# Key loads in 1 KB packets with head-wise turning, first scores in halves, and a re-ordered plan

## The chip, the cores and the metric

One core of one Trainium2 chip runs the program. The metric is the device time of one execution in microseconds (us). Lower is better. The kernel before was timed three times: 790.86, 791.15 and 791.73 us, median 791.15.

## The reference

Three stages follow each other, all in float32.

```python
scores = scale * np.matmul(q, k.transpose(0, 1, 3, 2))      # q, k, v: (2, 8, 576, 64)
kth = np.partition(scores, -32, axis=-1)[..., -32:-31]
scores = np.where(scores >= kth, scores, -1000000000.0)
attn = np.exp(scores - np.max(scores, axis=-1, keepdims=True))
attn = attn / (np.sum(attn, axis=-1, keepdims=True) + 1e-09)
x = np.matmul(attn, v)                                      # -> (1152, 512)

p = domain_probs / (domain_probs.sum(-1, keepdims=True) + 1e-09)
for e in range(4):                                          # w1 (4, 512, 1024), w2 (4, 1024, 512)
    out += p[:, e:e + 1] * (np.maximum(x @ w1[e], 0.0) @ w2[e])

y = ((out @ w_a) * (out @ w_b)) @ w_out                     # (512, 1536), (512, 1536), (1536, 512)
```

Each row of scores keeps only its 32 largest entries. Then come four experts, all applied to all tokens, and a gated pair of matrix products.

## The kernel before, in words

The 1152 tokens are cut into nine tiles of 128. They form four groups of 1, 2, 3 and 3 tiles (`GROUPS`). Attention works in 36 **steps**: for each group, for each pair of heads, for each tile. Step 0 to 3 are the one tile of group 0, steps 4 to 11 the two tiles of group 1.

A step goes through these stages:

- **Scores** (`scores`, TensorE): four matmuls of 288 columns for two heads, into two PSUM slots (`atts`, two of them). ScalarE copies them to SBUF (L813).
- **Selection** (`masked`, VectorE): the 32 largest of each row, eight at a time, by MAX8 (L842) and MATCH_REPLACE8 (L859). Steps 0 to 11 fold the row into two halves of 288 columns first, the later steps work on 576.
- **Softmax** (`masked`): GpSimd makes the limits (L905, L909), ScalarE the mask (L915) and the exponential with its sum (L920), GpSimd adds 1e-9 to the two sums (L925), VectorE takes the reciprocal (L928), ScalarE scales (L931).
- **Turning** (`weigh`, TensorE, "the turn" below): after a small GpSimd memset (L950), nine transposes into both `atts` slots. ScalarE copies them out (L977).
- **Values** (`weigh`, TensorE, "AV" below): ten matmuls of 64 output rows for each tile, into PSUM bank 7 (`os_`). ScalarE (and VectorE, for the groups of several tiles) takes the result away as `xf` (group 0, L1005) or `xs` (L1011, L1013).

The rows of keys come by `keys`: one DMA for the main part of a pair of heads (four blocks of 128 rows), one load of the remaining rows for all heads, six transposes (L689) and one copy by ScalarE (L705). Keys of batch 0 are turned in the first 20 us, those of batch 1 (`keys(1, prep, n + 2.0)`) during steps 1 to 6, and are kept in DRAM for the later groups. The first key load has its own path: its block copies are split between ScalarE (L701) and VectorE (L702).

Between these, TensorE does the experts of the groups already attended (`plain` for group 0 in float32, `experts` for the others in split float32r) and at last the gated products (`gated`). Before any of this work exists, 150 **filler** matmuls on zeros (`FILL`, `ps<-xs 128x256`) stand in the holes. They write into an `ms` slot, one of three PSUM banks that group 0's experts also use, and hold it until the last of them.

The order in which each engine's instructions stand is fixed when the kernel is built. `Plan` is a list scheduler: every piece of work has an engine, an assumed duration, a **key** (the smaller goes first among the pieces that are ready), its waits and its buffers. `AHEAD` sets the key of the scores (`n - AHEAD`), `SLACK` is an assumed delay after the sums of the softmax, `SINCE` gives the earliest assumed time of group 0's four wide weight loads. The planner tries 42 orders with small random delays and keeps one. On the chip each engine takes its own instructions strictly in that order, and DMAs of SyncE (SP) are issued in order too.

Of the kernel before, what the change touches and what calls it, by code (L numbers as in the profile page):

```python
# [29 lines left out]

AHEAD = 4.4
OPERANDS = 5.0
# [361 lines left out]
def dve(n):  # L394
    return 62 + 1.04 * n
# [18 lines left out]
FILL = 150  # L414
SLACK, EASE = 1200, 600

# [10 lines left out]
EARLY, WIDE = 4, 4  # L427
SINCE = 20e3, 25e3, 30e3, 40e3


def body(tc, q, k, v, probs, w1, w2, wa, wb, wo, out):
# [227 lines left out]
    def keys(b, h2, key):  # L659

        h = 2 * h2
        rt, kt = kraws.tile(key), kts.tile(key)
        rv = lambda: rt.ap.rearrange("p (m h d) -> p m h d", h=2, m=M4)
        first_ = not krem_done
        lds = [load(rv, lambda: pair_rows(k, b, h), key - 2, (), [rt])]

# [12 lines left out]
        else:  # L679
            done = krem_done[0]  # L680
        at = atts.tile(key + 0.02)
        kr = lambda i: krem0[(1 - b, b)[i]].ap if first_ else krem[(1 - b, b)[i]].ap[:, h * D:(h + 2) * D]
        krs = krem0 if first_ else krem

        def turn(blocks):
            a = at.ap.rearrange("p c n -> p (c n)")
            for i in blocks:
                src = kr(i // (M4 + 1)) if i % (M4 + 1) == 0 else rt.ap[:, (i - 1) * 128:i * 128]
                tr(a[:, i * 128:(i + 1) * 128], src, ident)  # L689

        if first_:

            o = tensor(3 * TURN_F, lambda: turn((1, 2, 3)), key + 0.02, lds + [ready], [at, rt])
            o = tensor(TURN_F, lambda: turn((0,)), key + 0.021, [o, done[0], done[3]], [at] + krs)
            o2 = tensor(2 * TURN_F, lambda: turn((4, 5)), key + 0.022, [o] + done, [at, rt] + krs)
        else:
            o = tensor(6 * TURN_F, lambda: turn(range(M4 + 2)), key + 0.02, lds + done + [ready], [at, rt] + krs)
        av = lambda c0, c1: at.ap.rearrange("p c n -> p (c n)")[:, REM + c0:REM + c1]
        if first_:
            got = [  # L700
                scalar(512 - REM, lambda: nc.scalar.activation(kt.ap[:, 0:512 - REM], av(0, 512 - REM), AF.Copy), -902, [o], [at, kt]),  # L701
                vector(dve(2 * REM + 64), lambda: nc.vector.tensor_copy(kt.ap[:, 512 - REM:WK], av(512 - REM, WK)), -902, [o2], [at, kt]),  # L702
            ]
        else:
            got = [scalar(WK, lambda: nc.scalar.activation(kt.ap, av(0, WK), AF.Copy), -902, [o], [at, kt])]  # L705
        if any(c for c, g in enumerate(GROUPS) if (b, h2) not in kept and c >= 0):
# [9 lines left out]
    def queries(pair, n, key):  # L716
# [19 lines left out]
        if MIX in pair.tiles:  # L736
# [3 lines left out]
            lds += qrem_done  # L740
        at = ms.tile() if n == 0 else atts.tile(key + 0.04)
        a = lambda: (at.ap if n == 0 else at.ap[:, 0])[:, 0:T * 128]
# [49 lines left out]
    def scores(pair, i, n):  # L792

        t = pair.tiles[i]
        ats, ss_ = [atts.tile(n - AHEAD + 0.001 * j) for j in range(2)], [scores_slot(n + 0.001 * j * (1 if n else -1)) for j in range(2)]
        parts = [(slice(0, 128), t[0])] if t != MIX else [(slice(b * REM, (b + 1) * REM), b) for b in range(B)]

        def emit():
            for c in range(2):
                for j in range(2):  # L800
                    for rs, b in parts:
                        c0 = (1 - j) * REM + c * HALF
                        mm(
                            ats[j].ap[rs, c, 0:HALF], pair.q.ap[j * D:(j + 1) * D, i * 128 + rs.start:i * 128 + rs.stop],
                            pair.k[b].ap[j * D:(j + 1) * D, c0:c0 + HALF], start=True, stop=True,
                        )

        o = tensor(SCORE / 2 + TILED, emit, n - AHEAD, pair.qd + sum((pair.kd[b] for _, b in parts), []), ats + [pair.q] + [pair.k[b] for _, b in parts])
        got = []
        for j in range(2):  # L810
            at, s = ats[j], ss_[j]
            ev = scalar(
                S, lambda s=s, at=at: nc.scalar.activation(s.ap.rearrange("p (c n) -> p c n", c=2), at.ap[:, :, 0:HALF], AF.Copy),  # L813
                -2000 + n, [o], [at, s],
            )
            got.append((s, ev, at, o))
        return got

    def masked(sd, n):
# [91 lines left out]
        for x in range(2):  # L911
# [12 lines left out]
            ))  # L924
        sm = gpsimd(290, lambda: nc.gpsimd.tensor_scalar(sums.ap, sums.ap, 1e-9, None, op0=ALU.add), -500, ex, [sums])  # L925

# [11 lines left out]
    def weigh(pair, i, ed, n):  # L938
# [46 lines left out]
        def emit():  # L985
# [11 lines left out]
        pair.od = [tensor(  # L997
            T * AV + SWITCH, emit, n + 0.6, [zeroed] + sum((d for _, _, d in pair.turned), []) + sum((pair.vd[b] + vrem_done[b] for b in bs), []),
            [pair.o] + [p for _, p, _ in pair.turned] + [pair.v[b] for b in bs],
# [491 lines left out]

    idle = ms.tile()
    steps = [(c, h2, i) for c, g in enumerate(GROUPS) for h2 in range(HP) for i in range(len(g))]
# [11 lines left out]
    for i in range(FILL):  # L1505
        late = i >= 150
        op = tensor(
            120, lambda: mm(idle.ap[:, 0:256], zeros_[:, 0:128], zeros_[:, 128:384], start=True, stop=True),
            1e9 + i, [blank], [idle],
        )  # L1510
# [33 lines left out]
```

## Time and profile before

| what | us |
|---|---|
| median of three runs | 791.15 |
| the profiled execution's own time | 791.33 |
| span of its profile, first to last instruction | 789.5 |
| TensorE (PE) busy | 779.3 |
| VectorE (DVE) busy | 710.3 |
| ScalarE (ACT) busy | 504.6 |
| GpSimd (POOL) busy | 324.3 |

The profiled execution's time is 1.8 us above its span and 0.18 us above the median. A busy PE is not a PE at its peak: matmuls are pipelined and overlap, so what one costs is read from the distance between the starts of equal ones and not from its own length. A float32 matmul of the program appears as two in the profile.

### The profile page before, as it was taken

Reading aid. Unit: us, or ns where it says so; the run is one execution under the profiler, and the core shown is the slowest. Engines: PE = TensorE matmul, PEld = TensorE weight load, DVE = VectorE, ACT = ScalarE, POOL = GpSimd, SP = SyncE. Lnnn points to the kernel's source line nnn. Section 1 sums busy time; section 2 is a strip of 40 time slices with the busy share of each in tenths; the row PEclk is TensorE's granted clock in tenths of the full one; section 3 lists DMA queues with packets and bytes.
Section 4 is the critical chain, followed back from the end, with each engine's and each line's share of the span. In section 5 each row is a group of like instructions: output and inputs, shape, how many; then the busy total and the mean of one; then the engine's idle time right before and its main releaser. Section 6 shows DMA issues by size and latency. Waiting matters only on the chain.

```text
span 789.5 us, 14542 instructions
## 1 busy us (share of the span) xinstructions
PE 779.3 (99%) x5286; PEld 684.7 (87%) x5286; DVE 710.3 (90%) x1548; ACT 504.6 (64%) x871; POOL 324.3 (41%) x353
## 2 busy tenths in 40 slices
PE   9989999999999999999999999999999999999997
PEld 8877676888888888889998999998898989999896
DVE  6999999999999999999939998999786899898655
ACT  3888888999888898787765566666436424241010
POOL 4354423568575534546445122232314424343120
PEclk9999999999999999999999999999999999999999
DMA  6867976756556524324345558896311331311013
GB/s 157 257 221 240 304 213 207 216 170 186 156 166 186 168 71 134 107 82 135 106 160 161 177 163 315 275 321 216 107 54 54 107 103 59 107 54 54 1 54 120
DMA packets 99464, 121.35 MB, mean 154 GB/s; under 512 B 26560, under 2 KB 73664, under 8 KB 97856
## 3 DMA queue, kind: packets, MB, share of 16 engines
q1 hardware_dynamic: 98976, 120.33, 48.4%
q8 instruction: 41, 0.67, 0.3%
q14 instruction: 31, 0.25, 0.1%
q10 hardware_dynamic: 416, 0.10, 0.1%
HBM read 109.14 MB, written 11.27 MB: 153 GB/s over the span
## 4 chain that ended last, share of the span: by engine, by line
PE 75%; DVE 21%; DMA 1%; issue 1%; POOL 1%; ACT 0%; DVEq 0%; POOLq 0%; SPq 0%
PE ps L597 72%; DVE low L842 9%; DVE e L859 7%; PE ps L600 3%; DVE e L882 1%; DMA e<-in_moe_w_b_dram 1%; DMA raw<-in_moe_w_dram 0%; DVE rest L1440 0%; DVE low L1440 0%; POOL mid_again L1035 0%; DVE low L1387 0%; DVE mid_again L1107 0%; POOL rest L1443 0%; DVE low L893 0%; DVE big_again L1394 0%
## 5 line engine op out<-in xcount | busy, mean ns | idle before, releaser
L597 PE MATMUL ps<-mid_again 128*128 128x512 f32 x1092 | 261.4, 393 | 0.0
L597 PEld LDWEIGHTS ps<-mid_again 128*128 128x128 f32 x1092 | 201.6, 188 | 42.2 <-issue 1.6
L597 PE MATMUL ps<-xs,mid_again 128*128 128x384 f32 (+1 forms) x1152 | 192.2, 320 | 0.7 <-DVE mid_again L1107 0.7
L597 PEld LDWEIGHTS ps<-xs,mid_again 128*128 128x128 f32 x1152 | 181.3, 189 | 8.0 <-issue 4.7
L1035 POOL TENSOR_TENSOR mid_again<-raw,mid_again 128x1024 fp32r<-128x1024 f32 x64 | 154.1, 2415 | 50.5 <-ACT mid_again L1034 49.6
L842 DVE MAX8 low<-e 128x8 f32<-128x576 f32 (+1 forms) x285 | 160.7, 599 | 0.0
L1351 POOL TENSOR_TENSOR low<-e,e 128x512 int32<-128x512 int32 x36 | 61.3, 1702 | 146.2 <-DVE e L1348 85.5
L1034 ACT ACTIVATE mid_again<-raw 128x1024 fp32r<-128x1024 f32 x96 | 101.9, 1063 | 20.9 <-PE ps L597 11.2
L859 DVE MATCH_REPLACE8 e<-low,e 128x576 f32<-128x576 f32 (+1 forms) x190 | 112.0, 594 | 0.0
L597 PE MATMUL ps<-xs,big_again 128*128 128x320 f32 (+1 forms) x576 | 86.4, 297 | 0.1
L597 PEld LDWEIGHTS ps<-xs,big_again 128*128 128x128 f32 x576 | 80.4, 190 | 1.1 <-DVE low L1440 0.3
L597 PE MATMUL ps<-lowa_again,big_again 128*128 128x320 f32 (+1 forms) x432 | 66.7, 297 | 1.0 <-ACT rest L1449 0.8
L1103 ACT ACTIVATE mid_again<-ps 128x384 fp32r<-128x384 f32 (+1 forms) x96 | 43.8, 457 | 31.5 <-PE ps L597 30.0
L597 PEld LDWEIGHTS ps<-lowa_again,big_again 128*128 128x128 f32 x432 | 60.6, 190 | 2.6 <-ACT rest L1449 1.1
L931 ACT ACTIVATE e<-e,low 128x576 f32<-128x576 f32 x72 | 52.9, 773 | 11.7 <-DVE low L928 11.4
L920 ACT ACTIVATE e<-e,low 128x576 f32<-128x576 f32 x72 | 55.8, 779 | 0.2
L1107 DVE SCALAR_TENSOR_TENSOR mid_again<-ps,mid_again 128x384 fp32r<-128x384 f32 (+1 forms) x96 | 48.1, 502 | 7.2 <-ACT mid_again L1103 6.7
L1440 DVE TENSOR_TENSOR low<-ps,low 128x256 f32<-128x256 f32 (+1 forms) x105 | 43.5, 444 | 11.9 <-PE ps L597 11.4
L1443 POOL TENSOR_TENSOR low<-low 128x256 f32<-128x256 f32 (+1 forms) x30 | 28.5, 950 | 59.6 <-DVE low L1440 58.4
L597 PE MATMUL ps<-big 64*128 64x288 f32 (+1 forms) x320 | 46.6, 427 | 1.7 <-ACT lowa L977 1.7
L977 ACT ACTIVATE lowa<-ps 128x512 f32<-128x512 f32 x72 | 42.8, 646 | 5.0 <-PE ps L600 4.9
L1035 DVE TENSOR_TENSOR mid_again<-raw,mid_again 128x1024 fp32r<-128x1024 f32 x32 | 40.7, 1277 | 4.3 <-ACT mid_again L1034 3.9
(125 smaller groups left out, 1101.5 us busy)
## 6 DMA issues: line engine op xcount, KB each, us to landing
raw<-in_moe_w_dram SPq DMA_DIRECT2D x116, 512.0 KB, 4.0
low<-in_v_dram SPq DMA_DIRECT2D x24, 256.0 KB, 3.5
e<-in_moe_w_b_dram SPq DMA_DIRECT2D x12, 512.0 KB, 3.8
e<-in_moe_w_a_dram SPq DMA_DIRECT2D x12, 512.0 KB, 4.1
e<-in_moe_w_out_dram SPq DMA_DIRECT2D x12, 512.0 KB, 5.2
wscr<-big_again SPq DMA_DIRECT2D x6, 1024.0 KB, 7.3
mid_again<-wscr SPq DMA_DIRECT2D x6, 1024.0 KB, 4.8
big<-kscr SPq DMA_DIRECT2D x16, 320.0 KB, 3.3
```

The lines of the kernel that those rows point to most:

```text
L597: nc.tensor.matmul(out, l, r, **kw)
L842: 62 + 1.04 * width, lambda at=at, cs=cs: nc.vector.max(m8v()[:, x, cs], at()), key + 0.02 * r, done if isinstance(done, list) else [done],
L859: lambda at=at, cs=cs, to=to: nc.vector.match_replace(out=to(), in_to_replace=m8v()[:, x, cs], in_values=at(), imm_value=LOW),
L920: lambda x=x: nc.scalar.activation(ev(x), ev(x), AF.Exp, bias=endv()[:, x, 0:1], accum_out=sums.ap[:, x:x + 1]),
L931: S, lambda x=x: nc.scalar.activation(ev(x), ev(x), AF.Copy, scale=sums.ap[:, x:x + 1]),
L977: w, lambda j=j, w=w, at=at: nc.scalar.activation(p.ap[:, j * MAIN:j * MAIN + w], at.ap.rearrange("p b n -> p (b n)")[:, j * (MAIN - 128): ...
L1034: hi = scalar(1024, lambda: nc.scalar.activation(u.ap[:, 0:1024], r.ap, AF.Copy), 500 + s, [ld], [u, r], sbuf=True)
L1035: sub = lambda eng: eng.tensor_tensor(u.ap[:, 1024:2048], r.ap, u.ap[:, 0:1024], op=ALU.subtract)
L1103: n, lambda h=h, p=p: nc.scalar.activation(h.ap[:, 0:n], p.ap[:, 0:n], AF.Relu), -1000, [o], [h, p]
L1107: lambda h=h, p=p: nc.vector.scalar_tensor_tensor(h.ap[:, n:2 * n], p.ap[:, 0:n], 0.0, h.ap[:, 0:n], op0=ALU.max, op1=ALU.subtract),
L1351: return gpsimd(pool_(512), lambda: nc.gpsimd.tensor_tensor(t().bitcast(I32), fold(c.ap.bitcast(I32)), fold(lowv().bitcast(I32)), op=ALU.a ...
L1440: return vector(dve(m), lambda: nc.vector.tensor_tensor(tv(out), p.ap[:, 0:m], tv(i), op=ALU.add), K, [o] + after, [p, tp])
```

## The change

- The main part of a pair of keys is loaded head by head, `main_rows` in place of `pair_rows`. Four rows of one head lie together in DRAM, so a packet is 1 KB instead of 256 B.
- In the new layout a block's two heads do not lie side by side. So each of the four main blocks is turned by two matmuls against the identity, one for each head, that write 64 rows each, in place of one transpose of 128 rows. The two blocks of remaining rows keep their transpose.
- For the first keys the turned blocks lie in two `ms` slots, not in an `atts` slot.
- Step 0's scores are two pieces: the first 288 columns wait for ScalarE's copy of the first keys alone, the second for VectorE's too.
- The sum gets its 1e-9 by a ScalarE activation (L936 in the new numbering) instead of a GpSimd instruction, at the key of its neighbours.
- Fillers write into the unused half of bank 7 and hold no slot.
- Numbers of the planner: scores 4.7 steps ahead (4.4), `SLACK` 600 (1200), `SINCE` of the second to fourth wide load 23, 26, 33 thousand (25, 30, 40), AV at `n + 0.55` (0.6).

```diff
-AHEAD = 4.4
+AHEAD = 4.7
-SLACK, EASE = 1200, 600
+SLACK, EASE = 600, 600
-SINCE = 20e3, 25e3, 30e3, 40e3
+SINCE = 20e3, 23e3, 26e3, 33e3
...
-        rv = lambda: rt.ap.rearrange("p (m h d) -> p m h d", h=2, m=M4)
+        rv = lambda: rt.ap.rearrange("p (h m d) -> p h m d", h=2, m=M4)
-        lds = [load(rv, lambda: pair_rows(k, b, h), key - 2, (), [rt])]
+        lds = [load(rv, lambda: main_rows(k, b, h), key - 2, (), [rt], 100 << 10 if first_ else 200 << 10)]
...
-        at = atts.tile(key + 0.02)
+        ats_ = [ms.tile(-1.0), ms.tile(-1.0)] if first_ else [atts.tile(key + 0.02)]
...
             for i in blocks:
-                src = kr(i // (M4 + 1)) if i % (M4 + 1) == 0 else rt.ap[:, (i - 1) * 128:i * 128]
-                tr(a[:, i * 128:(i + 1) * 128], src, ident)
+                c = slice(i % M4 * 128, (i % M4 + 1) * 128) if first_ else slice(i * 128, (i + 1) * 128)
+                if i % (M4 + 1) == 0:
+                    tr(a[:, c], kr(i // (M4 + 1)), ident)
+                    continue
+                for j in range(2):
+                    mm(a[j * D:(j + 1) * D, c], rv()[:, j, i - 1], ident, start=True, stop=True)
...
-        o = tensor(SCORE / 2 + TILED, emit, n - AHEAD, pair.qd + sum((pair.kd[b] for _, b in parts), []), ats + [pair.q] + [pair.k[b] for _, b in parts])
+        used = ats + [pair.q] + [pair.k[b] for _, b in parts]
+        if n:
+            o = tensor(SCORE / 2 + TILED, emit, n - AHEAD, pair.qd + sum((pair.kd[b] for _, b in parts), []), used)
+        else:
+
+            kd = pair.kd[t[0]]
+            o = tensor(SCORE / 4 + TILED / 2, lambda: emit((0,)), n - AHEAD, pair.qd + kd[:1], used)
+            o = tensor(SCORE / 4 + TILED / 2, lambda: emit((1,)), n - AHEAD, [o] + kd, used)
...
-        sm = gpsimd(290, lambda: nc.gpsimd.tensor_scalar(sums.ap, sums.ap, 1e-9, None, op0=ALU.add), -500, ex, [sums])
+        sm = scalar(2, lambda: nc.scalar.activation(sums.ap, sums.ap, AF.Copy, bias=1e-9), ks, ex, [sums], sbuf=True, extra=100)
...
-    idle = ms.tile()
+    idle = ps[:, 7, 256:512]
```

Over the whole program TensorE gets 32 instructions more, ScalarE 36 more, GpSimd 36 fewer. VectorE and the DMA queues keep theirs, in another order. Three places show how the planner's order moves.

TensorE from the matmuls before step 3's turn (nine transposes from `e_4_694`, in the change from `e_4_730`) on. `xf,mid` are group 0's expert matmuls, `big 128x288` a step's scores, `lowa` AV, `identr,big` the turning of keys and queries. Before:

```order
L597 MATMUL ps<-xf,mid 128x128 x12
L600 MATMUL ps<-identr,e_4_694 128x128 x9
L597 MATMUL ps<-big 128x288 x4
L597 MATMUL ps<-lowa,low 64x128 x8
L597 MATMUL ps<-lowa,rest 64x128 x2
L600 MATMUL ps<-identr,big 128x128 x6
```

and in the change:

```order
L597 MATMUL ps<-xf,mid 128x128 x2
L597 MATMUL ps<-big 128x288 x4
L597 MATMUL ps<-xf,mid 128x128 x10
L600 MATMUL ps<-identr,e_4_730 128x128 x9
L600 MATMUL ps<-identr,big 128x128
L597 MATMUL ps<-identr,big 64x128 x8
L600 MATMUL ps<-identr,big 128x128
L597 MATMUL ps<-lowa,low 64x128 x8
```

The turning of a pair of keys stands right behind the turn now, ahead of AV and scores, and scores moved ahead of the turn: nine blocks of scores are issued before step 3's turn where there were eight.

VectorE around step 0's reciprocal (`e_1_202`, in the change `e_1_206`, is step 1, the next tile name step 2). Before:

```order
L859 MATCH_REPLACE e_1_202<-low,e_1_202 128x288 x2
L842 MAX low<-e_1_202 128x8 x2
L842 MAX low<-e_1_256 128x8
L928 RECIPROCAL low<-low 128x2
L893 TENSOR_TENSOR low<-low 128x2x16
```

and in the change:

```order
L870 MATCH_REPLACE e_1_206<-low,e_1_206 128x288 x2
L939 RECIPROCAL low<-low 128x2
L853 MAX low<-e_1_206 128x8 x2
L853 MAX low<-e_1_264 128x8
L904 TENSOR_TENSOR low<-low 128x2x16
```

The reciprocal moved ahead of three MAX8.

TensorE around the last turn of all, step 35 (`e_26_4260`, in the change `e_28_4303`). `xs,mid_again 128x384` and `mid_again 128x512` are matmuls of the experts of group 2. Before:

```order
L597 MATMUL ps<-mid_again 128x512 x33
L597 MATMUL ps<-xs,mid_again 128x384 x30
L600 MATMUL ps<-identr,e_26_4260 128x128 x9
L597 MATMUL ps<-xs,mid_again 128x384 x9
L597 MATMUL ps<-lowa,low 64x128 x8
```

and in the change:

```order
L597 MATMUL ps<-mid_again 128x512 x15
L597 MATMUL ps<-xs,mid_again 128x384 x42
L600 MATMUL ps<-identr,e_28_4303 128x128 x9
L597 MATMUL ps<-xs,mid_again 128x384 x6
L597 MATMUL ps<-mid_again 128x512 x3
L597 MATMUL ps<-lowa,low 64x128 x8
```

Behind the turn 18 matmuls of 384 columns were left of this expert half (nine before AV, nine after), now six; the 36 of 512 columns that follow are the same number. So twelve of 384 columns moved ahead of the last turn.

## Rows read from the trace of the kernel before

**Rows 1.** The page: busy time of each engine, share of the span, instructions.
```profile
PE 779.3 (99%) x5286; PEld 684.7 (87%) x5286; DVE 710.3 (90%) x1548; ACT 504.6 (64%) x871; POOL 324.3 (41%) x353
```

**Rows 2.** Busy time by stretch: PE, weight loads, DVE, ACT, POOL; clock, DMA share, GB/s.
```profile
50.00:60.00 10.00, 9.05 (x91) 7.63 (x91) 10.00 (x39) 9.09 (x19) 5.41 (x11) 1.00 0.46 110
...
140.00:160.00 20.00, 19.78 (x136) 17.01 (x135) 20.00 (x45) 20.00 (x38) 13.49 (x12) 1.00 0.67 198
...
450.00:500.00 50.00, 50.00 (x255) 45.62 (x254) 47.17 (x73) 32.87 (x50) 12.97 (x7) 1.00 0.68 231
```

**Rows 3.** The chain that ended last, 150 to 165 us: start, length, what.
```profile
158.06 4.53 PE ps L597 x30
```

**Rows 4.** What PE waited for in the whole span: us, times, longest.
```profile
PE ps L597 <- ACT lowa L977: 1.7, 3, 1.0
...
PE ps L597 <- ACT xf L1005: 0.4, 1, 0.4
```

**Rows 5.** Timeline 3 to 9 us, PE, ACT and DVE: start, length, instruction.
```profile
4.40 0.90 PE L600 MATMUL ps<-identr,big 128*128 128x128 f32 x3
...
5.10 0.42 PE L600 MATMUL ps<-identr,low 128*128 128x128 f32 x1
...
5.56 0.54 ACT L701 ACTIVATE big<-ps 128x448 f32<-128x448 f32 x1 [2.36 <-PE ps L600]
...
5.98 0.36 DVE L702 COPY big<-ps 128x192 f32<-128x192 f32 x1 [2.07 <-PE ps L600]
...
6.73 1.30 PE L597 MATMUL ps<-big 64*128 64x288 f32 x8
...
8.13 0.77 DVE L837 MAX8 low<-ps 128x8 f32<-128x576 f32 x1 [1.79 <-PE ps L597]
```

**Rows 6.** The page: DMA issues, KB each, median us to landing.
```profile
low<-in_v_dram SPq DMA_DIRECT2D x24, 256.0 KB, 3.5
...
big<-in_k_dram SPq DMA_DIRECT2D x8, 256.0 KB, 3.6
```

**Rows 7.** Busy time in two stretches with a full DMA share.
```profile
3.20:4.40 1.20, 1.20 (x6) 0.94 (x5) 0.29 (x1) 0.00 (x0) 0.03 (x1) 1.00 0.96 215
80.00:100.00 20.00, 20.00 (x142) 13.78 (x141) 20.00 (x75) 16.88 (x33) 9.07 (x17) 1.00 0.92 306
```

**Rows 8.** Timeline of PE, 50 to 60 us: keys, experts, step 3's turn, scores.
```profile
51.30 1.09 PE L600 MATMUL ps<-identr,big 128*128 128x128 f32 x8
52.23 2.84 PE L597 MATMUL ps<-xf,mid 128*128 128x128 f32 x24
54.96 0.97 PE L600 MATMUL ps<-identr,e 128*128 128x128 f32 x9
56.89 1.83 PE L597 MATMUL ps<-big 64*128 64x288 f32 x8 [0.95 <-ACT lowa L977]
58.65 1.09 PE L597 MATMUL ps<-lowa,low 128*64 128x128 f32 x16
59.57 0.39 PE L597 MATMUL ps<-lowa,rest 128*64 128x128 f32 x4
```

**Rows 9.** Timeline of DVE at step 0's reciprocal.
```profile
26.67 0.80 DVE L842 MAX8 low<-e 128x8 f32<-128x288 f32 x2
27.39 0.15 DVE L928 RECIPROCAL low<-low 128x2 f32<-128x2 f32 x1
```

**Rows 10.** Groups of ACT instructions by line and form: busy us, mean ns.
```profile
L920 ACT ACTIVATE e<-e,low 128x576 f32<-128x576 f32 x72 | 55.8, 779 | 0.2
...
L920 ACT ACTIVATION_READ_ACCUMULATOR e<-e,low 128x1 f32 x72 | 14.6, 202 | 0.0
```

**Rows 11.** What ACT waited for.
```profile
ACT e L931 <- DVE low L928: 11.4, 12, 1.9
```

**Rows 12.** Timeline of PE before the last turn.
```profile
400.34 5.39 PE L597 MATMUL ps<-xs,mid_again 128*128 128x384 f32 x30
...
405.56 0.89 PE L600 MATMUL ps<-identr,e 128*128 128x128 f32 x9
```

More of the change, by code (lines that the diff above doesn't have):

```diff
@@ L685, in turn @@
         def turn(blocks):
-            a = at.ap.rearrange("p c n -> p (c n)")
+            a = ats_[blocks[0] // M4 % len(ats_)].ap
+            a = a if first_ else a.rearrange("p c n -> p (c n)")
             for i in blocks:
-                src = kr(i // (M4 + 1)) if i % (M4 + 1) == 0 else rt.ap[:, (i - 1) * 128:i * 128]
-                tr(a[:, i * 128:(i + 1) * 128], src, ident)
+                c = slice(i % M4 * 128, (i % M4 + 1) * 128) if first_ else slice(i * 128, (i + 1) * 128)
[4 more added lines that the diff above has]
+                    mm(a[j * D:(j + 1) * D, c], rv()[:, j, i - 1], ident, start=True, stop=True)
@@ L691, in keys @@
         if first_:
-            o = tensor(3 * TURN_F, lambda: turn((1, 2, 3)), key + 0.02, lds + [ready], [at, rt])
-            o = tensor(TURN_F, lambda: turn((0,)), key + 0.021, [o, done[0], done[3]], [at] + krs)
-            o2 = tensor(2 * TURN_F, lambda: turn((4, 5)), key + 0.022, [o] + done, [at, rt] + krs)
-        else:
-            o = tensor(6 * TURN_F, lambda: turn(range(M4 + 2)), key + 0.02, lds + done + [ready], [at, rt] + krs)
-        av = lambda c0, c1: at.ap.rearrange("p c n -> p (c n)")[:, REM + c0:REM + c1]
+            o = tensor(3 * TURN_F, lambda: turn((1, 2, 3)), key + 0.02, lds + [ready], [ats_[0], rt])
@@ L699, in keys @@
+            o = tensor(TURN_F, lambda: turn((0,)), key + 0.021, [o, done[0], done[3]], ats_[:1] + krs)
+            o2 = tensor(2 * TURN_F, lambda: turn((4, 5)), key + 0.022, [o] + done, [ats_[1], rt] + krs)
+        else:
+            o = tensor(6 * TURN_F, lambda: turn(range(M4 + 2)), key + 0.02, lds + done + [ready], ats_ + [rt] + krs)
         if first_:
             got = [
-                scalar(512 - REM, lambda: nc.scalar.activation(kt.ap[:, 0:512 - REM], av(0, 512 - REM), AF.Copy), -902, [o], [at, kt]),
@@ L702, in keys @@
-                vector(dve(2 * REM + 64), lambda: nc.vector.tensor_copy(kt.ap[:, 512 - REM:WK], av(512 - REM, WK)), -902, [o2], [at, kt]),
+                scalar(512 - REM, lambda: nc.scalar.activation(kt.ap[:, 0:512 - REM], ats_[0].ap[:, REM:512], AF.Copy), -902, [o], [ats_[0], kt]),
+                vector(dve(2 * REM + 64), lambda: nc.vector.tensor_copy(kt.ap[:, 512 - REM:WK], ats_[1].ap[:, 0:2 * REM + 64]), -902, [o2], [ats_[1], kt]),
             ]
         else:
-            got = [scalar(WK, lambda: nc.scalar.activation(kt.ap, av(0, WK), AF.Copy), -902, [o], [at, kt])]
+            got = [scalar(WK, lambda: nc.scalar.activation(kt.ap, ats_[0].ap.rearrange("p c n -> p (c n)")[:, REM:REM + WK], AF.Copy), -902, [o], [ats_[0], kt])]
@@ L740, in queries @@
             lds += qrem_done
-        at = ms.tile() if n == 0 else atts.tile(key + 0.04)
+        at = ms.tile(-2.0) if n == 0 else atts.tile(key + 0.04)
         a = lambda: (at.ap if n == 0 else at.ap[:, 0])[:, 0:T * 128]
@@ L796, in scores, with emit @@
         parts = [(slice(0, 128), t[0])] if t != MIX else [(slice(b * REM, (b + 1) * REM), b) for b in range(B)]
-        def emit():
-            for c in range(2):
+        def emit(cs=(0, 1)):
+            for c in cs:
                 for j in range(2):
@@ L997, in weigh @@
         pair.od = [tensor(
-            T * AV + SWITCH, emit, n + 0.6, [zeroed] + sum((d for _, _, d in pair.turned), []) + sum((pair.vd[b] + vrem_done[b] for b in bs), []),
+            T * AV + SWITCH, emit, n + 0.55, [zeroed] + sum((d for _, _, d in pair.turned), []) + sum((pair.vd[b] + vrem_done[b] for b in bs), []),
             [pair.o] + [p for _, p, _ in pair.turned] + [pair.v[b] for b in bs],
@@ L1507, in body @@
         op = tensor(
-            120, lambda: mm(idle.ap[:, 0:256], zeros_[:, 0:128], zeros_[:, 128:384], start=True, stop=True),
-            1e9 + i, [blank], [idle],
+            120, lambda: mm(idle, zeros_[:, 0:128], zeros_[:, 128:384], start=True, stop=True),
+            1e9 + i, [blank], [],
         )
```

## The prediction

> **What bounds the kernel now.** I read the busy times of the engines first, then the busy time by stretch, then the chain of waits, then what TensorE waited for.
>
> The page gives TensorE 99% and VectorE 90% of the span [rows 1]. A share over the whole span hides two stages. By stretch, VectorE is busy all the time in the attention stage, and TensorE is nearly so: from 50 to 60 us 10.00 of 10 against 9.05, from 140 to 160 us 20.00 of 20 against 19.78. Later, from 450 to 500 us, TensorE is full (50.00 of 50) and VectorE is not (47.17) [rows 2]. The chain that ended last says where the one hands over to the other: up to about 157 us it consists of VectorE's selection almost alone, and from 158.06 us on of matmuls [rows 3]. What TensorE waited for in the whole span is short: the longest entry is 1.7 us in three waits for ScalarE's copies after a turn, and 0.4 us in one wait for the copy of `xf` [rows 4].
>
> So the time has two parts. In the first 57 us TensorE has little useful work, since the experts of group 0 wait for the first four steps, and these come as fast as VectorE and the chain behind it let them. After that TensorE always has something to do. **An edit changes the time only in two ways: it lets the stretch of full work begin earlier or later, or it changes how much TensorE work is left at that point.** Work added to VectorE, ScalarE or GpSimd is worth nothing unless it moves one of these. The boundary is step 3's turn at 54.96 us: the scores behind it still waited 0.95 us for ScalarE's copies, at 56.89 us, and from there on the matmuls follow each other [rows 8].
>
> **The start.** The first keys take part in a chain of load, turning, two copies, scores and first MAX8. It has three changes.
>
> - The load. The keys move in 256 B packets, and at a DMA share of 0.96 the queue moved 215 GB/s; in a stretch of larger packets, at a share of 0.92, it moved 306 GB/s [rows 7]. I scale the second to the first share: 319 GB/s. 262 KB then take 0.82 us, not 1.22: a gain of 0.40 us. The median times to landing say less: 3.5 us for the values, which have 1 KB packets, and 3.6 us for the keys [rows 6], so 0.1 us is the lower end; 0.5 us more than the value taken is my upper end, in case the transfers beside it (queries, remaining keys) get out of the way as well.
> - A rule speaks about the same step. The Trainium skill, "DMA: Bandwidth & Descriptors", section "Why small descriptors are slow (HBM only)", gives each packet three bus cycles beside its bytes, so 11 for 256 B and 35 for 1 KB. An estimate by that page: 1024 packets take 11264 cycles and 256 packets 8960, which would shorten 1.22 us by a fifth, 0.25 us, and the sum below would be 0.15 us worse. The two stretches of the trace differ by a third [rows 7], more than the page's fifth.
> - The turning. At 4.40 us three transposes start within 0.70 us, 0.23 us each [rows 5]; at 51.30 us eight start within 0.93 us, 0.116 us each [rows 8]. The granted clock of the early stretch reads 1.00 [rows 7], but its spacing is that of the lower level, 1.2 GHz. What two 64-row matmuls cost is not in this stretch. The nearest rows are AV's: eight 64-row matmuls of the program start within 0.92 us (58.65 to 59.57) [rows 8], 0.115 us each, the price of a whole transpose. So a turned block costs twice as much: three blocks ahead of ScalarE's copy cost 6 x 0.23 us instead of 3 x 0.23, a loss of 0.69 us.
> - The scores in halves. Before, the scores at 6.73 us followed VectorE's copy, which ended at 6.34; ScalarE's ended at 6.10 [rows 5]. The first half no longer waits for the later one: a gain of 0.24 us. The second half comes 0.65 us later (half of 1.30 us), by when VectorE's copy is through.
>
> Together -0.40 + 0.69 - 0.24 = **+0.05 us**, between -0.5 and +0.4. I take 0: VectorE starts its selection at 8.13 us as before.
>
> **TensorE's work at the boundary.** Twelve of the 32 extra matmuls' blocks lie behind step 3's turn: three pairs of keys of batch 1, four blocks each. By the AV row a pair costs 4 x 0.115 = 0.46 us more: **+1.4 us**. The other five pairs (four in the first 20 us, one behind step 2's turn) lie where fillers or waits stood, and cost the end nothing; were that cover gone they would cost 5 x 0.46 = 2.3 us. `AHEAD` works the other way: nine blocks of scores stand ahead of step 3's turn instead of eight, and a block lasts 1.30 us [rows 5], so **-1.3 us** is no longer left behind the boundary. The two nearly cancel.
>
> **The wait behind the turn.** The order now puts the turning of a pair of keys between step 3's turn and its AV and scores. It takes eight 64-row matmuls and two transposes, 10 x 0.115 = 1.15 us, and needs nothing from that turn. So the 0.95 us wait [rows 8] is filled: **-0.95 us**. If the keys land late it stays.
>
> **The reciprocals.** Step 0's reciprocal passes three MAX8. Two of them start within 0.72 us (26.67 to 27.39) [rows 9], so it comes 1.1 us earlier; steps 1 to 3 gain 0.4 to 1.6 us in the same way. ScalarE did wait for reciprocals, 11.4 us in 12 waits [rows 11]. But the boundary moves only if TensorE gets there too. In the new order fillers, AV, a block of scores, twelve expert matmuls and the next turn follow each other, and ScalarE has an exponential (0.78 + 0.20 us [rows 10]) and another step's copies ahead of the copies that AV waits for. I take 0 for the place of step 3's turn, from -0.4 (what its own reciprocal gains) to +0.9 us (one exponential that AV or the first expert matmul has to wait out).
>
> **ScalarE's addition.** No row has a 128x2 activation. The nearest is the 128x1 read of the accumulator, 0.20 us [rows 10]; 36 of them are 7.3 us, and GpSimd loses as many instructions. ScalarE is full from 140 to 160 us [rows 2], where two of them fall. I take 0 on the path, with 8 x 0.2 = 1.6 us as the upper end for the crowded stretch from 120 to 200 us. The Trainium skill, "ScalarE: Activation LUTs", section "Rules for kernel authors", budgets about 0.3 us for each activation with a bias operand; the trace's smallest, 0.20 us, lies below that. An estimate by that page is 10.8 us of ScalarE instead of 7.3, and the upper end would be 2.4 us. The other edits (fillers without a slot, `SINCE`, the key of AV) only show in the order, and the count above includes them.
>
> **Sum:** 0 + 1.4 - 1.3 - 0.95 + 0 = **-0.85 us**. Against the profiled execution's 791.33 us that is 790.5; against the median, 0.18 us lower, 790.3. I round the change to -0.9 and forecast **790.2 us**.
>
> **A count from the other end** checks it. Behind the last turn twelve matmuls of 384 columns fewer are left. Thirty took 5.22 us (400.34 to 405.56) [rows 12], so that is -2.1 us, if the last turn stays at 405.56. VectorE has up to three more expert additions ahead of the last selection, about 2 us by the order, and the wait for GpSimd and ScalarE behind it may take that up in part: the last turn comes 0 to 2.0 us later. The end moves by -2.1 to -0.1 us, which holds the sum.
>
> **Rivals.**
>
> - **The early reciprocals come through** and the boundary moves. Then step 3's turn is about 1 us earlier (the mean gain of the four steps), and the other waits of the first steps shrink as well, 1.7 - 0.95 + 0.4 = 1.2 us [rows 4]. -0.85 - 1.0 gives -1.9 us, with all of the waits -3.0: about 788.3 us. For it: ScalarE really waited on them. Against it: the new order gives TensorE more to do ahead of each early turn.
> - **The keys stand in the way** and it gets slower. Between a turn and its AV now lie 1.15 us of key turning, so AV, the copy of `xf` and the expert matmuls behind it come later; ScalarE has two exponentials and a key copy to do before that `xf`. TensorE would stand still behind AV, where it waited 0.4 us once [rows 4]. With 0.8 us in each of four steps, +3.2 us, the sum is +2.3: 793.5 us. It decides from about 2.4 us of new waits between 35 and 80 us.
> - **The load does not get faster**, as its time to landing suggests [rows 6]. Then the start loses 0.35 us: 790.6 us, which nobody could tell from the forecast.
>
> **How the numbers follow.** A measurement of this kernel tells 0.2% from no change, 1.6 us here: below 789.6 is faster, above 792.7 slower. The forecast has a chance of 0.44, with a range of its own from 789.6 to 792. The first rival has 0.38, the second 0.15, the third 0.03. Faster is the first rival's 0.38, the same is the forecast's and the third's 0.47, slower the second's 0.15. The range reaches to the first rival's -1.9 us with the -0.5 us of the start and a little of its waits, -3.2, and up to +1.8, where the second begins: 788.0 to 792.9.
>
> **What would show it.** Right: first MAX8 within 0.4 us of 8.13; the first key turning's 64-row matmuls 0.2 us apart, later ones 0.115; no wait of TensorE for the copies behind step 3's turn; step 3's turn between 54.5 and 55.9 us; the last turn between 405 and 408 us; matmuls without a gap behind it. Wrong: a first MAX8 below 7.6 us, a step 3's turn below 54 us (first rival) or above 57 us with TensorE waiting for `xf` (second), or waits of over 2 us behind the last turn, which the order there gives no reason for.

## The result, and the profile after

Five executions of the changed kernel took 795.31 to 797.13 us, median **795.42**; five of the kernel before on the same chip 790.86 to 791.73, median 791.1. The ratio is 1.0056, 95% interval 1.0044 to 1.0067: slower by 4.4 us, where the prediction had 790.2 us and 792.9 as the end of its range. The profiled execution of the changed kernel was the longest, 797.13 us with a span of 795.3; a second profile, from a later run, has 795.0 and the same picture.

The page of the changed kernel, busy time of each engine, against [rows 1]:

```profile
PE 784.9 (99%) x5382; PEld 687.9 (86%) x5382; DVE 713.6 (90%) x1548; ACT 510.2 (64%) x907; POOL 317.9 (40%) x317
```

TensorE's busy time grew by 5.6 us, VectorE's by 3.3. The page's summary of the chain that ended last, before:

```profile
PE 75%; DVE 21%; DMA 1%; issue 1%; POOL 1%; ACT 0%; DVEq 0%; POOLq 0%; SPq 0%
```

and the changed kernel:

```profile
PE 90%; DVE 7%; ACT 1%; issue 1%; DMA 0%; POOL 0%; DVEq 0%; POOLq 0%
```

Long pieces of that chain at its start, changed kernel: start, length, what. Before, it left TensorE at 8.1 us, with the first scores, and VectorE's selection made up almost all the rest of the first 157 us [rows 3]. Now its first link is the query's load, and TensorE's queue holds it up to step 0's turn at 35.10 us: the piece at 28.48 us is 34 fillers and two blocks of scores. VectorE has it from there to 57 us, ScalarE to 61.7 us, and then TensorE again.

```profile
0.74 3.49 DMA big<-in_q_dram
4.81 1.91 PE ps L597 x14
...
8.15 3.99 PE ps L597 x19
...
14.72 3.14 PE ps L597 x23
...
19.36 3.64 PE ps L597 x27
...
28.48 6.79 PE ps L597 x50
...
36.35 1.44 DVE e L893 x2
```

The start, changed kernel, timeline of PE, ACT and DVE from 4 to 11 us, against [rows 5]:

```profile
4.36 0.45 PE L600 MATMUL ps<-identr,big 128*128 128x128 f32 x1 [0.97 <-DMA big<-in_q_dram]
...
5.16 1.55 PE L597 MATMUL ps<-identr,big 128*64 128x128 f32 x12
...
6.64 0.48 PE L600 MATMUL ps<-identr,low 128*128 128x128 f32 x1
7.05 0.70 PE L597 MATMUL ps<-identr,big 128*64 128x128 f32 x4
7.16 0.54 ACT L705 ACTIVATE big<-ps 128x448 f32<-128x448 f32 x1 [3.87 <-PE ps L600]
7.68 0.48 PE L600 MATMUL ps<-identr,low 128*128 128x128 f32 x1
...
8.51 2.29 PE L597 MATMUL ps<-big 64*128 64x288 f32 x8
...
10.84 0.77 DVE L848 MAX8 low<-ps 128x8 f32<-128x576 f32 x1 [2.29 <-PE ps L597]
```

One 64-row matmul leaves two records 0.007 us apart, so x12 are six matmuls. The first MAX8 is at 10.84 instead of 8.13 us, and the scores take 2.29 us instead of 1.30 [rows 5].

The boundary, changed kernel, timeline of PE from 58 to 66 us, against [rows 8]:

```profile
60.19 0.96 PE L600 MATMUL ps<-identr,e 128*128 128x128 f32 x9
61.75 0.33 PE L600 MATMUL ps<-identr,big 128*128 128x128 f32 x1 [0.61 <-ACT lowa L988]
62.01 1.09 PE L597 MATMUL ps<-identr,big 128*64 128x128 f32 x16
63.04 0.33 PE L600 MATMUL ps<-identr,big 128*128 128x128 f32 x1
63.30 1.09 PE L597 MATMUL ps<-lowa,low 128*64 128x128 f32 x16
64.22 0.39 PE L597 MATMUL ps<-lowa,rest 128*64 128x128 f32 x4
```

Step 3's turn moved from 54.96 to 60.19 us. The wait behind it is still there, 0.61 us instead of 0.95, and it is now the key turning that waits for ScalarE's copies. From step 3's turn to the end it is 735.1 us (795.3 - 60.19); before, 734.5 (789.5 - 54.96).

So three numbers read from each trace place a loss: the **first MAX8**, from there **to step 3's turn**, and from there **to the end of the span**. Before: 8.13, 46.83 and 734.5 us. The changed kernel: 10.84, 49.35 and 735.1; in its second profile (e13 below) 10.61, 49.30 and 735.1.

### The profile page after: what moved, and what is told of

The parts are those of the page before. It is cut to its first block, busy times and chain, and to the rows that moved or that the text cites. A ratio compares the mean times of both kernels' runs of the same rounds, so it can differ in the third digit from the quotient of the medians.

```text
span 795.3 us, 14747 instructions
## 1 busy us (share of the span) xinstructions
PE 784.9 (99%) x5382; PEld 687.9 (86%) x5382; DVE 713.6 (90%) x1548; ACT 510.2 (64%) x907; POOL 317.9 (40%) x317
## 4 chain that ended last, share of the span: by engine, by line
PE 90%; DVE 7%; ACT 1%; issue 1%; DMA 0%; POOL 0%; DVEq 0%; POOLq 0%
PE ps L597 86%; PE ps L600 4%; DVE low L853 1%; DVE e L870 1%; DVE low L1451 1%; DVE rest L1451 1%; DVE big_again L1405 1%; DVE e L893 0%; DMA big<-in_q_dram 0%; DVE mid_again L1472 0%; DVE e L1356 0%; POOL rest L1454 0%; DVE mid_again L1118 0%; ACT e L942 0%; ACT e L926 0%
## 5 line engine op out<-in xcount | busy, mean ns | idle before, releaser
L988 ACT ACTIVATE lowa<-ps 128x512 f32<-128x512 f32 x72 | 42.8, 646 | 6.2 <-PE ps L600 6.0
```

What stands on the lines that cost most here:

```text
L988: w, lambda j=j, w=w, at=at: nc.scalar.activation(p.ap[:, j * MAIN:j * MAIN + w], at.ap.rearrange("p b n -> p (b n)")[:, j * (MAIN - 128): ...
```

## The experiments

Each was timed against the kernel before on its own chip; that median is 791.78 for e1 to e4, 791.43 for e5 to e9, 791.67 for e10 to e13, 791.58 for e14 to e17. "New keys" are 1 KB packets with 64-row matmuls.

| kernel | us | ratio to before (95%) | first MAX8 | to step 3's turn | to the end |
|---|---|---|---|---|---|
| e1 old keys, new order | 790.72 | 0.9988 (0.9979 to 0.9997) | 8.31 | 47.35 | 732.9 |
| e2 first pair old | 794.62 | 1.0037 (1.0024 to 1.0051) | 7.52 | 49.96 | 734.9 |
| e3 keys behind the query | 796.53 | 1.0050 (1.0035 to 1.0066) | 7.94 | 49.27 | 735.1 |
| e4 sum on GpSimd | 798.83 | 1.0086 (1.0072 to 1.0100) | 10.39 | 49.23 | 737.9 |
| e5 27 fillers fewer | 795.14 | 1.0056 (1.0043 to 1.0070) | 10.17 | 47.93 | 735.3 |
| e7 e1, 12 fillers fewer | 790.71 | 0.9990 (0.9981 to 0.9999) | 8.32 | 46.65 | 733.2 |
| e8 old order, new keys | 797.15 | 1.0078 (1.0066 to 1.0091) | 10.59 | 48.33 | 736.5 |
| e9 e1, last three pairs new | 793.29 | 1.0016 (1.0007 to 1.0025) | 8.86 | 47.62 | 735.1 |
| e10 remainder ahead of keys | 796.75 | 1.0061 (1.0049 to 1.0074) | 10.42 | 50.28 | 735.1 |
| e11 e1, scores 4.4 ahead | 791.07 | 0.9997 (0.9988 to 1.0005) | 8.89 | 46.72 | 735.6 |
| e12 e1, first pair new | 793.49 | 1.0019 (1.0009 to 1.0028) | 10.62 | 48.13 | 733.1 |
| e13 the changed kernel | 796.86 | 1.0066 (1.0053 to 1.0080) | 10.61 | 49.30 | 735.1 |
| e14 old packets, new turning | 796.67 | 1.0061 (1.0049 to 1.0074) | 10.30 | 50.08 | 735.1 |
| e15 e1, first pair's turning new | 792.09 | 1.0004 (0.9996 to 1.0013) | 9.04 | 46.96 | 733.0 |
| e16 e1, operands 5.2 ahead | **790.10** | 0.9979 (0.9970 to 0.9988) | 8.42 | 46.69 | 733.5 |
| e17 e1, scores 4.5 ahead | 793.27 | 1.0023 (1.0013 to 1.0033) | 8.86 | 47.43 | 735.6 |

The last three columns are of one profiled execution each. Kernels timed on different chips are best compared by their ratios; the first MAX8 also depends on when TensorE's clock reached its higher level, which differed between executions (last section).

### Keys, order, or addition (e1 to e4)

e1 keeps the changed kernel's order and gives the keys their old form. e2 does this for the first pair alone.

```
-  rv = ... rearrange("p (h m d) -> p h m d", ...)      main_rows(k, b, h)
+  rv = ... rearrange("p (m h d) -> p m h d", ...)      pair_rows(k, b, h)
-  for j in range(2): mm(a[j * D:(j + 1) * D, c], rv()[:, j, i - 1], ident, ...)
+  tr(a[:, c], rt.ap[:, (i - 1) * 128:i * 128], ident)
```

> The changed kernel, with its order on every engine, but all keys are loaded in 256 B packets and turned by whole transposes as before the change. Theory A (the start: the 1 KB packets hold up the query, the 64-row matmuls run at the lower clock level, and TensorE carries the lost 2.7 us on): first MAX8 at 8.0 to 8.8 us instead of 10.84, step 3's turn at 55 to 57 us instead of 60.19, time 789 to 792. Theory B (the planner's new order costs it, whatever the packets): step 3's turn at 58 us or later, time 794 or more. Between 792 and 794 both have a share.

> As e1_old_keys for the first pair of keys alone; the other seven pairs keep 1 KB packets and 64-row matmuls. Theory A says that the first pair makes the loss: first MAX8 at 8.0 to 8.8 us, time within 0.8 us of e1_old_keys. If the four later turnings of the first 25 us make it (theory D: 64-row matmuls and the gaps on either side of them fill TensorE's in-order queue), first MAX8 is as early but step 0's turn still is over 33 us, and the time is 793.5 or more. Theory B: as after, 794.5 or more.

e1 is 1.06 us faster than before: **the whole loss lies in the keys' new form**, and the rest of the change, order and addition together, gains a little. Theory B falls. Before, four fillers stood between the first turning and the scores:

```profile
5.60 1.20 PE L597 MATMUL ps<-xs 128*128 128x256 f32 x4
```

The start of e1, timeline of PE and DVE, against the changed kernel's above:

```profile
4.49 0.90 PE L600 MATMUL ps<-identr,big 128*128 128x128 f32 x3 [0.46 <-DMA big<-in_k_dram]
5.19 0.42 PE L600 MATMUL ps<-identr,low 128*128 128x128 f32 x1
...
6.39 1.88 PE L597 MATMUL ps<-big 64*128 64x288 f32 x8
...
8.31 0.77 DVE L847 MAX8 low<-ps 128x8 f32<-128x576 f32 x1 [1.88 <-PE ps L597]
```

But e2 is not e1: with the first MAX8 as early as 7.52 us it still takes 794.62. Theory A, as put (the first pair makes the loss), falls too; seven other pairs cost 3.9 us (1.0037 against 0.9988). That is theory D's time; its sign, step 0's turn over 33 us, was just missed (32.40).

e3 issues the first keys on ScalarE's queue behind the query; e4 adds 1e-9 on GpSimd in the same place.

```
-  nc.sync.dma_start(rt, main_rows(k, b, h))       (SyncE, first)
+  nc.scalar.dma_start(rt, main_rows(k, b, h))     (ScalarE, behind the query)

-  nc.scalar.activation(sums.ap, sums.ap, AF.Copy, bias=1e-9)
+  nc.gpsimd.tensor_scalar(sums.ap, sums.ap, 1e-9, None, op0=ALU.add)
```

> The changed kernel with the first load of keys issued on ScalarE's queue behind the query's instead of on SyncE's beside it; nothing else moves. If the packets of the keys hold up the query (part of theory A), the query lands by 3.0 us instead of 4.22 and its transpose starts at about 3.2; the keys land 0.3 to 0.8 us later than 4.05. If the query's delay costs as much as it seems, first MAX8 comes 0.5 to 1.3 us earlier than 10.84 and the time falls to 794 to 795; if the 64-row turning at the lower level is the larger part, first MAX8 moves by less than 0.5 us and the time by less than 0.7 us.

> The changed kernel with 1e-9 added to the sums by GpSimd again, in the same place of every other engine's order. Theories A and B: within 0.6 us of the changed kernel's 795.4. Theory C (ScalarE has no room for 36 more instructions and the reciprocals that wait for them): 1 to 2.5 us faster, 793 to 794.4, and VectorE's waits for a sum (0.98 us at 74.6) are gone.

In e3 the query landed at 2.61 us and the keys at 4.13, and the profiled execution, 794.06 us, was the fastest; the median is 796.53, so the start gains nothing reliable: 0.5 to 1.3 us by the ratios (1.0050 against 1.0056 and 1.0066), with intervals that overlap. In e4 theory C missed by its sign, and theories A and B, which expected no change, missed too: the addition back on GpSimd costs 1.6 to 2.4 us more (1.0086 against 1.0066 and 1.0056), all of it behind step 3's turn (737.9 against 735.1). VectorE's reciprocal then waits for GpSimd, which fits; how this reaches TensorE was not followed. e4, what DVE waited for up to 420 us (total, times, longest):

```profile
DVE low L939 <- POOL low L936: 3.6, 6, 1.6
```

In the changed kernel the same reciprocal waited for ScalarE once:

```profile
DVE low L939 <- ACT low L936: 0.5, 1, 0.5
```

### Where the later pairs cost (e5 to e9)

```
e5, e7:  lambda: mm(idle, ...)  ->  lambda i=i: None if i in dropped else mm(idle, ...)
e5: every fourth of fillers 12 to 118 dropped     e7: e1, fillers 109 to 120 dropped
e8: the kernel before with main_rows(k, b, h), "p (h m d)" and the two 64-row matmuls per block
e9: e1, with the new keys only where b == 1 and h2 > 0
```

> The changed kernel without 27 of the 118 filler matmuls that stand ahead of step 0's turn (every fourth from the thirteenth on), 27 x 0.12 = 3.2 us of TensorE time; no other instruction moves. Theory D (before step 0's turn the split key matmuls lengthen TensorE's in-order queue, whose fillers leave no room, and so every result of TensorE's comes later): with the same first MAX8, step 0's reduction to its prelu shrinks from 2.6 to under 1.5 us, step 0's turn comes 1.5 to 3 us earlier than in the changed kernel's trace (35.10) and the time falls to 791.5 to 794. Rival (the delay comes from the copies and limits on ScalarE and GpSimd, not from TensorE's queue): step 0's turn within 0.7 us of its place and the time within 0.6 us of 795.4.

> e1_old_keys (old packets, whole transposes, new order) without the 12 filler matmuls directly ahead of and inside step 0's turn, which stood 1.44 us behind its cast there. If the early turns set when the full work begins, step 0's turn comes 1 to 1.4 us earlier (29.2 to 29.6), step 3's turn 0.5 to 1 us earlier than 55.66, and the time is 789.5 to 790.2. If step 3's turn is set by VectorE's selection and ScalarE's exponential between the two scalings (there its lag behind the cast was 0.06 us), it stays at 55.4 to 55.9 and the time at 790.5 to 791.

> The kernel before with its own order, numbers and slots; only the keys' packets (1 KB) and their turning in 64-row matmuls are new. If the keys' new form costs what it seems to in e1_old_keys against the changed kernel, whatever the order (theories A and D): 4 to 5 us slower than before, 795.5 to 797. If it only costs where the new order puts turnings between a turn and its AV, and the start: 1 to 2.5 us slower, 792.8 to 794.3.

> e1_old_keys with 1 KB packets and 64-row matmuls for the last three pairs of keys alone, which are turned behind step 3's turn. Priced by AV's rows, as the prediction had it, they add 1.4 us: 792.1. If each switch between whole transposes and 64-row matmuls costs 0.2 us more on either side, 3 x (0.46 + 0.4) = 2.6 us: 793.3, but the traces behind step 3's turn (735.1 us against 732.9 in e1_old_keys) say 2.1: 792.8. Step 3's turn stays at 55.4 to 56.0 in all cases.

e9 shows the price of a late pair. Timeline of PE behind step 3's turn in e1, whole transposes:

```profile
57.32 0.88 PE L600 MATMUL ps<-identr,big 128*128 128x128 f32 x6 [0.69 <-ACT lowa L987]
58.12 1.09 PE L597 MATMUL ps<-lowa,low 128*64 128x128 f32 x16
```

The same place in e9:

```profile
58.14 0.33 PE L600 MATMUL ps<-identr,big 128*128 128x128 f32 x1 [0.69 <-ACT lowa L992]
58.40 1.09 PE L597 MATMUL ps<-identr,big 128*64 128x128 f32 x16
59.43 0.33 PE L600 MATMUL ps<-identr,big 128*128 128x128 f32 x1
59.69 1.09 PE L597 MATMUL ps<-lowa,low 128*64 128x128 f32 x16
```

From the first transpose to AV it is 0.80 us in e1 and 1.55 us in e9: **0.75 us a pair**. In a run of their like, whole transposes and 64-row matmuls both start 0.109 us apart, so eight matmuls for four blocks instead of four transposes explain 0.44 us. The rest are switches of form, of which a pair has three instead of one: from a transpose to a 64-row matmul the starts are 0.26 us apart (58.14 to 58.40), and eight 64-row matmuls up to the next transpose take 1.03 us (58.40 to 59.43), where eight in a run take 0.87. The Trainium skill, "TensorEngine Tiling (Array Packing)", section "Tiling Modes", says that a change of tiling mode drains the engine; the trace agrees, with about 0.15 us for each. Three pairs: 2.2 us, and the end lies 735.1 instead of 732.9 us behind step 3's turn. The ratio says the same (0.0028, 2.2 us).

e8 shows that the old order pays as much (5.7 us). e5 and e7 ask how the early pairs reach the end. Step 0's limits follow its reduction on VectorE (at 21.72 us in e13, 19.92 in e1) on GpSimd, and its first activation follows on ScalarE. Timeline of GpSimd in the changed kernel (e13), 22 to 25 us:

```profile
22.19 1.78 POOL L889 TENSOR_TENSOR e<-big 128x288 int32<-128x288 int32 x2 [1.38 <-ACT big L824]
23.93 0.42 POOL L916 TENSOR_TENSOR low<-low,facs 128x4 f32<-128x4 f32 x1
```

and of ScalarE there:

```profile
21.46 1.19 ACT L824 ACTIVATE big<-ps 128x576 f32<-128x576 f32 x2 [1.59 <-PE ps L597]
24.14 0.71 ACT L709 ACTIVATE big<-ps 128x640 f32<-128x640 f32 x1 [1.48 <-PE ps L600]
...
24.90 1.44 ACT L926 ACTIVATE e<-lowa,low 128x576 f32<-128x576 f32 x2
```

The limits stand behind folds of a later step's scores, whose copies waited 1.59 us for TensorE; the activation stands behind a key copy, which waited 1.48 us for TensorE's turning. From the reduction to the activation it is 3.2 us, and 0.8 us in e1 (19.92 to 20.69). In e5, with 3.2 us of fillers fewer, it is 1.3 us, and step 3's turn comes 47.93 us behind the first MAX8 instead of 49.30. So in these traces TensorE's full queue passes the early pairs on as far as step 3's turn. Yet e5's median (795.14) is the rival's, not theory D's; its five executions spread from 794.50 to 797.87, and what its end gained is not settled. e7 moved step 3's turn by 0.7 us and the time not at all. That the early pairs cost time is measured (e2 less e9); that they do it through the fillers is shown up to step 3's turn only.

### Query, first pair and the new order's numbers (e10 to e13)

```
e10:  SyncE's first two loads exchanged: 64x2x64 remainder, then 128x2x256 keys
e11:  e1 with  AHEAD = 4.7  ->  AHEAD = 4.4
e12:  e1 with the new keys only for the first pair
e13:  the changed kernel, nothing edited
```

> The changed kernel with SyncE's first two loads in the other order (the 64-row remainder first, then the first pair's 1 KB packets), so that these packets start about 0.55 us later and the query has the engines to itself; nothing else moves. If the packets hold up the query and its wait is what the start loses: the query lands by 3.0 us instead of 4.22, the keys at 4.4 to 4.8 instead of 4.05, the wait of about 1 us ahead of the query's transpose is gone, and the time is 0.5 to 1.3 us below that of e13_after_again. If the start's loss is the 64-row matmuls at the lower clock level: first MAX8 within 0.4 us and the time within 0.5 us of e13_after_again.

> e1_old_keys with the scores 4.4 instead of 4.7 steps ahead, as before the change; the sums on ScalarE, the early reciprocals and all else stay, and the order is planned anew. The prediction's price for the block of scores that then stands behind step 3's turn: 1.3 us slower than e1_old_keys, 791.7 to 792.3. If the order with 4.4 lets AV follow its turn directly (the planner puts the key turnings into the experts' matmuls instead), the waits of 0.6 us behind the early turns go with it, step 3's turn is at 54.5 us or before, and the time is 789 to 790.5, below both kernels.

> e1_old_keys with 1 KB packets and 64-row matmuls for the first pair of keys alone. By the difference of e2_first_old and the changed kernel (0.8 to 1.5 us) 791.4 to 792.3, with the first MAX8 1.0 to 2.5 us later than 8.31 us. If the first pair only costs together with the next ones (TensorE's queue full): within 0.4 us of e1_old_keys, 790.3 to 791.1.

> The changed kernel itself, on the same chip as the other three, for their comparison. 795 to 796; its profiled execution before was the longest of five (797.13), so a typical one should have its first MAX8 at 9.0 to 10.2 us instead of 10.84 and the rest of the program unchanged behind it.

In e10 the query landed at 2.70 us and the keys at 4.71; TensorE then waited 0.72 us for the keys instead of 0.75 (e13) for the query, and the first MAX8 stayed at 10.42. So e10 exchanged one wait for another and does not price the query's delay; e3, where both landed early, leaves it at most about 1 us. e11 costs 0.4 us by the medians and 0.7 by the ratios (0.0009), less than the price expected, and the intervals overlap. e13 lies above the 795 to 796 expected, and its first MAX8 is late too, 10.61 us. e12 puts 2.5 us (ratio 0.0031) on the first pair alone, more than expected.

### Packets or turning (e14, e15), and a faster version (e16, e17)

```
e14:  the changed kernel, pair_rows(k, b, h) and "p (m h d)";
      mm(a[j * D:(j + 1) * D, c], rv()[:, i - 1, j], ident, ...)
e15:  the same for the first pair only, whole transposes for the others
e16:  e1 with  OPERANDS = 5.0  ->  5.2        e17:  e1 with  AHEAD = 4.7  ->  4.5
```

> The changed kernel with the keys in 256 B packets again, but still turned in 64-row matmuls: the change's turning without its packets. If the turning makes the loss (its matmuls, the switches on either side of them, the slow start behind them): 795.5 to 798, step 3's turn at least 48.5 us behind the first MAX8 and the end 735.1 us behind step 3's turn, as in the changed kernel. If the packets make it: 790.5 to 792.5.

> e1_old_keys with 64-row matmuls for the first pair of keys alone, in 256 B packets. Turning: as e12_first_new (793.49), 792.5 to 795, first MAX8 at 9.5 us or later, with the scores at half speed. Packets: as e1_old_keys, 790.3 to 791.3, first MAX8 under 9.2 us.

> e1_old_keys with the operands of a step due 5.2 instead of 5.0 steps ahead, planned anew: behind step 2's turn the key turning now stands behind AV and not between the two, behind step 3's turn it stays. An attempt at a faster version: the wait of 0.6 us behind one early turn goes, 789.5 to 790.5; if the planner's other moves weigh more, 791 to 792.

> e1_old_keys with the scores 4.5 steps ahead, planned anew: the scores of the early steps stand ahead of AV, the key turnings behind both, so nothing of the keys stands between an early turn and its AV. Theory: step 3's turn at 54.5 to 55.5 us, its end 733 to 734.5 us behind it, 789.5 to 790.5; if one block of scores fewer ahead of step 3's turn weighs as the prediction has it (1.3 us), 791.5 to 792.3.

e14 settles it for the eight pairs together: **the turning in 64-row matmuls makes the loss; the packets neither add nor save anything that can be told** (1.0061 between the two timings of the changed kernel, 1.0056 and 1.0066, with intervals of about 1 us either way). e15 missed both of its ranges: 792.09 lies between them, 1.3 us above e1 and 1.2 below e12 by the ratios (0.0016 and 0.0015), with intervals that touch on either side. So for the first pair alone the share of the packets is open. e14's chain begins with the keys' load, 256 B packets, and the turning:

```profile
0.74 3.86 DMA big<-in_k_dram
...
4.64 1.55 PE ps L597 x12
6.18 0.41 PE ps L600
6.59 0.63 PE ps L597 x4
7.22 0.41 PE ps L600
```

In e13 the same keys in 1 KB packets took 3.10 us to land, 0.76 us less, but the query beside them took 3.27 instead of e14's 1.99, and the query's transpose stands ahead of the key turning in TensorE's queue: the turning began at 4.94, in e14 at 4.64. The Trainium skill, "DMA: Bandwidth & Descriptors", section "Issuing engines are not separate DMA queues", says that loads issued by different engines run on the same 16 DMA engines and interleave; these two landings agree.

e16 is faster than both kernels, by 0.21% (0.12 to 0.30). What it does behind the early turns was only partly as expected: behind step 2's turn nothing waits for a key turning any more, behind step 3's the wait is 0.83 us. e17 came out slower than either range (793.27): step 3's turn at 56.29 us, the end 735.6 us behind it; the cause was not sought.

## Why the prediction was wrong

It had -0.85 us, measured are +4.4. Term by term, with e1 (new order, old keys) as the middle:

| term | predicted | measured |
|---|---|---|
| the start (first pair) | 0 (-0.5 to +0.4) | +2.5 (e12 against e1) |
| four pairs under "fillers or waits" | 0 | +1.7 (e2 less e9, ratio 0.0021) |
| three later key pairs | +1.4 | +2.2 (e9 against e1) |
| score block more, wait filled, reciprocals, addition | -2.25 | -0.9 (e1, ratio 0.9988) |

- **The start.** Two steps failed here. From e1's first MAX8 at 8.31 to e13's at 10.61 are 2.30 us (e13's start has the changed kernel's rows above, 0.22 us earlier). The first failed step is the load's gain of 0.40 us: the keys did land earlier, at 3.84 us instead of 4.45, but the query beside them at 4.01 instead of 2.72, and its transpose and two fillers stand ahead of the turning. So the turning begins 0.45 us later, 4.94 instead of 4.49. Three blocks take 1.48 instead of 0.70 us, +0.78 where the prediction had +0.69: right. The second is "the first half no longer waits for the later one: a gain of 0.24 us". There was no such wait: before, VectorE's copy ended at 6.34 us, and TensorE came to the scores at 6.73, behind four fillers. TensorE takes its queue in order, and one remainder block, the last two blocks and two fillers stand ahead of the first scores in it: 1.87 us instead of 1.20, a loss of 0.67. Halving a wait gains nothing when other work stands ahead in the same queue. The last 0.40 us are the scores, slower because the clock's higher level came late. They are chance and no price of the new form: e9, e11 and e17, with the first pair's old form, have the same slow scores and a first MAX8 at 8.86 to 8.89, so that 1.7 us of the start are left.
- **"The other five pairs ... cost the end nothing."** This step failed too; the four besides the first cost 1.7 us, about what the prediction gave without cover (4 x 0.46). Fillers are no cover in a queue taken in order: they are issued whether there is time or not, and 0.75 us more of key turning pushes the later results. The rows show whom: score copies and a key copy on ScalarE, folds on GpSimd, and behind these step 0's limits and activations.
- **Three later pairs.** The mechanism was right, the size not: 0.75 us each, not 0.46, since AV's rows show 64-row matmuls among their like and not the switches around them, 0.3 us a pair.
- **"Needs nothing from that turn."** Wrong. The key turning writes one of the two `att` slots in PSUM, and step 3's turn sits in one until ScalarE has copied it (L988). So a wait stayed, 0.61 us behind step 3's turn instead of 0.95; e1 has 0.69.
- **One block of scores more.** e1 has 1.6 us less behind step 3's turn than before (732.9 against 734.5), about the -1.3 predicted and the 0.3 that the wait lost, but step 3's turn lies 0.7 us later (55.66 against 54.96): part of it is only moved. e11 says 0.4 to 0.7 us net, on an order planned anew.
- **The reciprocals** did not move the boundary, as forecast: step 0's scaling waited for score copies that wait for TensorE, in e1 too.
- **ScalarE's addition.** The group of its rows, changed kernel (total us, mean ns):

```profile
L936 ACT ACTIVATE low<-low 128x2 f32<-128x2 f32 x36 | 7.5, 208 | 0.4
```

  208 ns against the 0.20 us taken from [rows 10]; the larger estimate beside it, 0.3 us, was too high. On the path it gains in this order (e4), where the prediction had 0 to +1.6.
- **The count from the other end** failed as well. From the last turn to the end it is 383.2 us instead of 383.9: 0.7 us less, not 2.1. TensorE waits 1.03 us for VectorE at 433.31 us, before 0.46, and later twice 0.19. The last turn lies at 412.10 us, 6.5 us later instead of 0 to 2.
- **The rivals.** "The keys stand in the way" had the sign and the place, turnings between a turn and its AV, but another mechanism: not waits for `xf` but work and switches, and TensorE waited no more than before. Its 15% was far too little: all eight pairs got dearer in ways that reach the end, and three were charged.

The measured terms sum to +5.5 us; the changed kernel's two timings are +4.4 and +5.2. The terms overlap at the early pairs (e12 also puts 0.8 us between first MAX8 and step 3's turn). Taken from the other side, the changed kernel less e2, the first pair is worth 1.5 to 2.3 us and not 2.5, so the share of each there is open to about 1 us.

## What to carry to other kernels

Price a change of form on TensorE with its switches, not with the spacing inside a run of like matmuls. Do not count fillers in an in-order queue as slack: here work added there delayed the later results, and the readers of these (copies on ScalarE, with a step's limits and activations behind them) showed by how much. A load that lands earlier is worth nothing if another one that has to be used first lands later.

## What was not expected of the hardware

Two executions with the same instructions up to 9 us, e14 and e15, ran the same four matmuls of scores (eight records) at different speeds. Timeline of PE, e14 and then e15:

```profile
7.98 2.29 PE L597 MATMUL ps<-big 64*128 64x288 f32 x8
```

```profile
7.76 1.24 PE L597 MATMUL ps<-big 64*128 64x288 f32 x8
```

By their spacing inside the run, 0.48 and 0.24 us, the first ran at the lower level (1.2 GHz) and the second at the higher (2.4 GHz); the granted clock of both stretches reads 1.00. TensorE had been busy since about 4.5 us in both; it had stood still for the keys 0.60 us in e14 and 0.39 in e15. The form of the first pair's keys does not decide it: e9, e11 and e17 have the old form and 2.29 us, as have e10, e12 and e13 with the new one, while before, e2 (old), e3, e8 and e15 (new) have 1.24 to 1.34. So the start can come about 1 us earlier or later with the same instructions. This may be part of the spread of e12's eleven times, 791.56 to 795.08, but only one of them was profiled. What decides the moment was not tried.
